# Resetting, at each batch item, the tally that shares PSUM evictions between ACT and DVE

## Chip, cores, metric

One core of a Trainium2 chip. The metric is the device time of one execution in microseconds (us), the median of several.

PE is TensorE, PEld its weight loads, DVE VectorE, ACT ScalarE, POOL GpSimd. "L581" in a profile line is a line of the program; where an experiment adds lines to the program, the same statement has a number a few higher or lower.

## The reference

Four batch items of 8 heads, 768 positions, head size 64. A Sinkhorn-normalised matrix P (8 by 8 per head) mixes blocks of K and V; block-local attention follows; its result goes through a two-branch layer:

```python
k_sorted = einsum('bhij,bhjcd->bhicd', P, k_b); v_sorted = einsum(... P, v_b)
attn = softmax(scale * q_b @ k_sorted^T)          # 96 x 96 blocks
x = (attn @ v_sorted) -> (B*S, H*D)               # 3072 x 512
out = maximum(x @ w1, x @ w2) @ w_out             # d_ff 1024
```

The kernel uses max(a, b) = max(a - b, 0) + b, so a hidden tile h needs a ReLU, and the second term becomes a product with wc = w2 @ w_out.

## The kernel before, where it matters

All matmul outputs, of every kind, use one PSUM pool of four buffers of 128 x 1024 fp32. Most evictions (PSUM to SBUF) may run on ACT or on DVE. `load` is a tally of estimated ns per engine, and `pick` takes the engine whose sum would be the lower. Work that is bound to one engine is added too.

```python
psum = ctx.enter_context(tc.tile_pool(name="psum", bufs=4, space=PSUM))  # 128 x 1024 fp32 each
load = {"A": 0.0, "D": 0.0}

def pick(a_ns, d_ns):
    if load["A"] + a_ns <= load["D"] + d_ns:
        load["A"] += a_ns
        return "A"
    load["D"] += d_ns
    return "D"

def evac(out_ap, in_ap, n, two_x=False, eng=None):
    a_ns, d_ns = (200 + n) / 1.2, (130 + (n / 2 if two_x else n)) / 0.96
    if eng:
        load[eng] += a_ns if eng == "A" else d_ns
    if (eng or pick(a_ns, d_ns)) == "A":
        nc.scalar.copy(out=out_ap, in_=in_ap)
    else:
        nc.vector.tensor_copy(out=out_ap, in_=in_ap)
# scores():  load["A"] += 800 (exp);  values(): load["D"] += 900;  turn(): load["D"] += 800
# moe_h():   the same pick, then a ReLU on ACT or a max on DVE
```

Items are pipelined: while item b goes through the hidden layer and the output product, item b+1 has its K and V sorted, its scores made and its attention applied. The loop of items (cut):

```python
for b in range(B):
    units = [lambda t=t: moe_h(b, 0, t, None if b else "A") for t in range(4)]
    ...                                   # the units of item b: h tiles, then outputs
    steps, lo = [], 2
    if b < B - 1:
        ...                               # the steps for item b+1: sort_k, sort_v, scores, values
        elif b == 1:
            vs = [lambda t=t: sort_v_pair(2, t) for t in range(8)]
            steps = group(*ks) + group(*vs[:2]) + group(*SC[0:2], late_loads)
            steps += group(*vs[2:4]) + group(*vs[4:6]) + group(*vs[6:]) + group(*SC[2:4]) + VA[:2]
    ...                                   # units and steps are issued in turn
```

Item 1 is thus where three K tiles and eight V tiles (V1 to V8) fall between eight h tiles. That stretch is what this document is about; its length is taken from the first K matmul to the first output matmul.

The softmax here doesn't subtract the row's maximum and nothing guards it: scores larger than these inputs give would overflow.

## Time and profile before

| | before |
|---|---|
| time | 173.48 us (173.47 to 173.84, 3 runs) |
| span in the profile | 171.4 us |
| TensorE busy | 161.7 us, 94% |
| ACT / DVE busy | 83.7 / 87.9 us |
| first K matmul to first output matmul of item 1 | 76.91 to 91.08: 14.17 us |

TensorE is busy 94% of the span, and a change that only moves evictions does not change its work, so only its waits can be won. Here is the end of the stretch, from the timeline of the kernel before (start, length, engine, line, operation):

```profile
91.08 1.25 PE L608 MATMUL out_ps<-wo_sb,g 128*128 128x512 bf16 x5
```

### The profile page before, as it was taken

Reading aid. Unit: us, or ns where it says so; the run is one execution under the profiler, and the core shown is the slowest. Engines: PE = TensorE matmul, PEld = TensorE weight load, DVE = VectorE, ACT = ScalarE, POOL = GpSimd, SP = SyncE. Lnnn points to the kernel's source line nnn. Section 1 sums busy time; section 2 is a strip of 40 time slices with the busy share of each in tenths; the row PEclk is TensorE's granted clock in tenths of the full one; section 3 lists DMA queues with packets and bytes.
Section 4 is the critical chain, followed back from the end, with each engine's and each line's share of the span. In section 5 each row is a group of like instructions: output and inputs, shape, how many; then the busy total and the mean of one; then the engine's idle time right before and its main releaser. Section 6 shows DMA issues by size and latency. Waiting matters only on the chain.

```text
span 171.4 us, 4548 instructions
## 1 busy us (share of the span) xinstructions
PE 161.7 (94%) x2015; PEld 96.6 (56%) x2015; DVE 87.9 (51%) x194; ACT 83.7 (49%) x102; POOL 24.8 (14%) x40
## 2 busy tenths in 40 slices
PE   7699999999999999998889999999999999999992
PEld 7548676736666554456555455575545445654462
DVE  5879668499556399810485644225472232420040
ACT  4599975846645554069764253275605214231001
POOL 7955362242300000000320000000000000000000
PEclk9999999999999999999999999999999999999999
DMA  4999999999999452992099267950023273000333
GB/s 49 201 205 207 199 207 206 207 205 207 213 222 196 76 168 54 193 232 96 4 174 189 54 168 145 195 183 4 2 50 77 91 205 130 6 0 0 122 122 126
DMA packets 29811, 23.11 MB, mean 135 GB/s; under 512 B 16672, under 2 KB 24736, under 8 KB 29792
## 3 DMA queue, kind: packets, MB, share of 16 engines
q0 software_dynamic: 10304, 12.58, 43.1%
q1 hardware_dynamic: 19200, 10.04, 23.2%
q8 instruction: 16, 0.26, 0.6%
q10 hardware_dynamic: 288, 0.20, 0.4%
q14 instruction: 3, 0.02, 0.0%
HBM read 25.17 MB, written 6.29 MB: 184 GB/s over the span
## 4 chain that ended last, share of the span: by engine, by line
PE 80%; DVE 10%; ACT 6%; issue 2%; DMA 1%; DVEq 0%; ACTq 0%
PE out_ps L608 37%; PE h_ps L581 22%; PE o_ps L471 4%; PE wc_ps L559 3%; PE k_ps L377 3%; PE s_ps L444 3%; ACT v_sb L103 2%; PE v_ps L398 2%; DVE v_sb L105 1%; ACT kT L103 1%; DVE x L488 1%; PE tw_ps L529 1%; PE tq_ps L347 1%; PE tq_ps L352 1%; ACT g L595 1%
## 5 line engine op out<-in xcount | busy, mean ns | idle before, releaser
L608 PE MATMUL out_ps<-wo_sb,g 128*128 128x512 bf16 (+2 forms) x208 | 48.3, 363 | 0.0
L581 PE MATMUL h_ps<-xT,w_sb 128*128 128x384 bf16 x256 | 44.8, 326 | 2.1 <-DVE v_sb L105 0.7
L581 PEld LDWEIGHTS <-w_sb 128*128 128x128 bf16 x256 | 24.2, 98 | 17.5 <-issue 2.0
L452 ACT ACTIVATE e<-s_ps 96x768 bf16<-96x768 f32 x32 | 24.2, 808 | 16.7 <-PE s_ps L444 16.6
L595 ACT ACTIVATE g<-h_ps 128x768 bf16<-128x768 f32 x23 | 18.6, 812 | 17.4 <-PE h_ps L581 17.4
L608 PEld LDWEIGHTS <-g 128*128 128x128 bf16 x208 | 17.6, 97 | 15.2
L608 PE MATMUL out_ps<-wc,xT 128*128 128x512 bf16 (+2 forms) x104 | 25.0, 362 | 0.0
L103 ACT COPY o<-out_ps 128x1024 f32<-128x1024 f32 x10 | 10.1, 1012 | 29.3 <-PE out_ps L608 24.7
L488 DVE TENSOR_TENSOR x<-o_ps,rs 96x512 bf16<-96x512 f32 x32 | 22.0, 687 | 1.1
L597 DVE TENSOR_SCALAR g<-h_ps 128x768 bf16<-128x768 f32 x9 | 8.6, 956 | 25.5 <-PE h_ps L581 25.5
L482 DVE RECIPROCAL rs<-o_ps 96x8 f32<-96x8 f32 x32 | 6.4, 200 | 21.4 <-PE o_ps L471 21.4
L608 PEld LDWEIGHTS <-xT 128*128 128x128 bf16 x104 | 9.9, 97 | 11.0
L471 PEld LDWEIGHTS <-e 96*128 96x128 bf16 x256 | 11.6, 98 | 6.9 <-DVE x L488 0.7
L209 DVE COPY v_dc<-v_raw 64x768 bf16<-64x768 bf16 (+2 forms) x18 | 15.4, 896 | 0.1
L471 PE MATMUL o_ps<-v_sb,e 96*128 96x65 bf16 x256 | 13.1, 193 | 0.3 <-DVE x L488 0.2
L105 DVE CAST v_sb<-v_ps 96x1024 bf16<-96x1024 f32 x7 | 8.3, 1214 | 4.1 <-PE v_ps L398 3.3
L103 ACT CAST v_sb<-v_ps 96x1024 bf16<-96x1024 f32 x9 | 8.8, 1020 | 1.6 <-PE v_ps L398 1.6
L444 PEld LDWEIGHTS <-kT 64*128 64x128 bf16 x256 | 6.1, 94 | 5.6 <-issue 4.8
L103 ACT CAST kT<-k_ps 128x1024 bf16<-128x1024 f32 x9 | 8.6, 1022 | 0.7 <-PE k_ps L377 0.7
L444 PE MATMUL s_ps<-qT,kT 64*128 64x96 bf16 x256 | 8.8, 204 | 0.2
L559 PE MATMUL wc_ps<-wo_sb,w2T 128*128 128x512 bf16 x32 | 7.7, 380 | 0.0
L81 PEld LDWEIGHTS <-fill 128*128 128x128 bf16 x109 | 6.3, 112 | 2.2 <-DVE fill L72 1.2
(76 smaller groups left out, 129.4 us busy)
## 6 DMA issues: line engine op xcount, KB each, us to landing
out_dram<-o SPq DMA_DIRECT2D x11, 512.0 KB, 3.0
k_raw<-in_k_dram POOLq DMA_DIRECT2D x12, 256.0 KB, 10.2
q_raw<-in_q_dram POOLq DMA_DIRECT2D x4, 768.0 KB, 12.5
v_raw<-in_v_dram POOLq DMA_DIRECT2D x6, 384.0 KB, 13.5
w_sb<-in_moe_w_dram POOLq DMA_DIRECT2D x3, 512.0 KB, 15.9
wo_sb<-in_moe_w_out_dram POOLq DMA_DIRECT2D x2, 512.0 KB, 19.2
v_raw<-in_v_dram POOLq DMA_DIRECT2D x3, 256.0 KB, 4.9
w_sb<-in_moe_w_dram POOLq DMA_DIRECT2D x2, 256.0 KB, 14.2
```

The lines of the kernel that those rows point to most:

```text
L103: nc.scalar.copy(out=out_ap, in_=in_ap)
L105: nc.vector.tensor_copy(out=out_ap, in_=in_ap)
L209: nc.vector.tensor_copy(out=dst, in_=src)
L444: nc.tensor.matmul(ps[:, h2 * 512 + ii * 128 : h2 * 512 + ii * 128 + BLK], kT[b][rows, (hp * 8 + i) * BLK : (hp * 8 + i) * BLK + 128], rhs ...
L452: nc.scalar.activation(out=e[:, 0 : 8 * BLK].rearrange("p (t c r) -> p t c r", t=8, r=R), in_=ps[0:BLK].rearrange("p (t f) -> p t f", t=8) ...
L471: nc.tensor.matmul(ps[:, h2 * 512 + ii * 65 : h2 * 512 + (ii + 1) * 65], e[:, (h2 * 4 + ii) * BLK : (h2 * 4 + ii) * BLK + 128], v_sb[:, m0 ...
L488: nc.vector.tensor_tensor(out=x, in0=ov[:, :, :, 0:D], in1=rs.to_broadcast([BLK, 2, 4, D]), op=ALU.mult,)
L559: nc.tensor.matmul(wc_ps[0][:, m * 512 : (m + 1) * 512], w2T[:, fb, dmt * 128 : (dmt + 1) * 128], wo_sb[:, fb, :], start=(fb == 0), stop=( ...
L581: nc.tensor.matmul(h_ps[t][:, m * 512 : m * 512 + TCH], w1_sb[:, hp, fb * 128 : (fb + 1) * 128], xT[:, b % 2, ch, hp % 2, hp // 2, :], sta ...
L595: nc.scalar.activation(out=g, in_=src, func=AF.Relu)
L597: nc.vector.tensor_scalar(out=g, in0=src, scalar1=0.0, scalar2=None, op0=ALU.max)
L608: nc.tensor.matmul(dst, g_tiles[b, ch, m // 2][:, m % 2, off : off + 128] if m < NFB else xT[:, b % 2, ch, hp % 2, hp // 2, off : off + 12 ...
```

## The change

The tally is meant to balance two engines, but it adds up from the start of the program, and a sum charged in one stage is paid back in another. The change starts it from zero at each item:

```diff
         steps, lo = [], 2
+        load["A"] = load["D"] = 0.0
         if b < B - 1:
```

No instruction is added; only which engine empties which tile changes. The choices of `pick` in order, before and after (A for ACT, D for DVE; those of item 0's tail, items 1, 2 and 3; the exps and copies that are bound to one engine are not among them):

```
item 0  before AAAAAADADADADDAAA        after AAAAAAAAADDADDAAA
item 1  before AAAAAAAAADDDAADADADAAA   after ADADADADADDADADAADAADA
item 2  before AAADADADADDAAA           after ADADADADADDAAA
item 3  before DADADAADAD               after ADADADADAD
```

## The prediction

> **What bounds the kernel now.** I read the page's first part, then the table of busy time by stretch, then what TensorE waited for, then the timeline of the one stretch in which TensorE isn't full. First the page: time busy, its share of the span, and instructions.
>
> ```profile
> PE 161.7 (94%) x2015; PEld 96.6 (56%) x2015; DVE 87.9 (51%) x194; ACT 83.7 (49%) x102; POOL 24.8 (14%) x40
> ```
>
> TensorE (PE) is the bound. The two engines that empty PSUM are half idle, so moving work between them gains nothing unless TensorE waits for one. TensorE idles 171.4 - 161.7 = 9.7 us. The table by stretch says where: per stretch its length, then busy us of PE, weight loads, DVE, ACT, POOL, the clock, DMA.
>
> ```profile
> 40.00:54.00 14.00, 13.65 (x244) 9.26 (x242) 8.96 (x11) 9.14 (x11) 1.44 (x2) 1.00 1.12 211
> 54.00:72.00 18.00, 18.00 (x180) 9.19 (x179) 14.22 (x30) 6.54 (x8) 0.00 (x0) 1.00 0.64 124
> 77.00:91.00 14.00, 12.07 (x296) 8.18 (x296) 5.83 (x6) 10.88 (x13) 2.67 (x5) 1.00 0.50 102
> 91.00:110.00 19.00, 19.00 (x178) 9.75 (x171) 8.76 (x19) 6.59 (x9) 0.00 (x0) 1.00 0.78 157
> 110.00:125.00 15.00, 14.64 (x220) 9.33 (x218) 6.20 (x9) 9.51 (x12) 0.00 (x0) 1.00 0.27 57
> ```
>
> From 54 to the output tail TensorE is full except from 77 to 91, where it lacks 1.93 us. There ACT is busy 10.88 of 14 us and DVE only 5.83: exactly the imbalance a tally should prevent. This is item 1 (the second of four): its hidden-layer tiles h, with item 2's sorted K (three tiles) and sorted V (eight) between them. The rest of the 9.7 us lies mostly ahead of 40 us (3.9 in the first two stretches of the same table) and after the last matmul, where no `pick` decides. TensorE's waits between 76.9 and 91.1:
>
> ```profile
> PE h_ps L581 <- DVE v_sb L105: 0.7, 1, 0.7
> PE h_ps L581 <- ACT v_sb L103: 0.6, 1, 0.6
> PE h_ps L581 <- ACT kT L103: 0.5, 1, 0.5
> ```
>
> These are matmuls waiting for an eviction unrelated to their operands: all PSUM tiles come from one pool of four buffers, so a tile starts when the tile four before it has been emptied. The timeline (start, length, what, idle before and its releaser) shows the queue behind it:
>
> ```profile
> 76.91 1.70 PE L377 MATMUL k_ps<-bd,k_raw 64*64 64x64 bf16 x96
> 77.01 0.81 ACT L595 ACTIVATE g<-h_ps 128x768 bf16<-128x768 f32 x1 [0.49 <-PE h_ps L581]
> 77.72 2.84 ACT L103 CAST kT<-k_ps 128x1024 bf16<-128x1024 f32 x3
> 79.69 1.46 PE L581 MATMUL h_ps<-xT,w_sb 128*128 128x384 bf16 x8 [0.51 <-ACT kT L103]
> 80.42 1.96 ACT L103 CAST v_sb<-v_ps 96x1024 bf16<-96x1024 f32 x2
> 82.42 1.46 PE L581 MATMUL h_ps<-xT,w_sb 128*128 128x384 bf16 x8 [0.57 <-ACT v_sb L103]
> 83.99 0.96 DVE L597 TENSOR_SCALAR g<-h_ps 128x768 bf16<-128x768 f32 x1 [10.25 <-PE h_ps L581]
> 84.87 3.47 DVE L105 CAST v_sb<-v_ps 96x1024 bf16<-96x1024 f32 x3
> 87.26 1.46 PE L581 MATMUL h_ps<-xT,w_sb 128*128 128x384 bf16 x8 [0.69 <-DVE v_sb L105]
> 114.43 2.36 DVE L105 CAST kT<-k_ps 128x1024 bf16<-128x1024 f32 x2 [6.19 <-PE k_ps L377]
> ```
>
> TensorE makes a K tile in 0.54 us (96 matmuls in 1.63 us, three tiles) and a V tile in 0.285 us (two in 0.57), but one eviction takes about 1.0 us on ACT or 1.2 on DVE. ACT takes nine evictions and two exps in a row while DVE idles 10.25 us; then DVE gets four in a row and TensorE waits for DVE. The last line is the same place one item later: there the tally was balanced, DVE took two of three K tiles, and TensorE did not wait.
>
> **Why the tally does this.** Each of item 0's turns of V charges DVE 800 ns, in a part of the kernel where TensorE does not wait. Worked through the code, the sums at the start of item 1 are ACT 35573, DVE 43021: a debt of 7447 ns, which ACT repays with the next nine picked evictions. For item 2 it is ACT 57013, DVE 58700; for item 3 ACT 71527, DVE 71110.
>
> **What the Trainium skill says.** "Perfetto Trace Analysis", Identifying the Most-Contended Engine, says that kernels can have regimes with different contended engines; the stretch table agrees (PE everywhere, evictions from 77 to 91). Its section Optimization Strategy says that the same gap repeating on the engine that should be saturated can mean too little PSUM for the next tile: three gaps of 0.5 to 0.7 us in 8 us, each released by an eviction, agree. "TensorEngine Tiling (Array Packing)", PSUM Bottleneck, advises using both ScalarE and VectorE for evacuation; the trace agrees that one alone can't keep up with 0.285 and 0.54 us tiles.
>
> **The change part by part.** It adds no instruction on the chip: both sums are set to zero while the program is built, at each item. The order of TensorE's instructions is identical. Only the engine of some evictions changes, found by comparing the built instruction orders; net, four go from ACT to DVE (DVE 183 to 187 counting sequencer rows).
>
> *Item 0's tail (43 to 53 us).* The reset comes before item 0's remaining picks, and DVE's charges lie ahead again: third K tile and second V tile go D to A, third V tile A to D. TensorE's two waits of 0.2 us there are for the first V tile's eviction and the weight product's copy, both on ACT as before. Gain 0. The moved V tile delays the Q copy on DVE by about 0.4 us, to end near 50.95; scores need it at 51.21. Cost 0.
>
> *Item 1's middle (73 to 91 us).* Engines, before then after, in tile order: h h h K K K V V h s s h V V h V V h V V h: A A A A A A A A A A A D D D A A D A D A D, becomes A D A D A D A D A A A D D A D A D A A D A. I replay it with durations from the trace: ACT h 0.81, K 1.02, V 1.00, exp 0.78; DVE h 0.96, K 1.19, V 1.2; ready 0.2 us after the last matmul; a buffer restarts 0.05 us after its eviction.
> - K1 on DVE 77.65 to 78.84, K2 on ACT 78.19 to 79.21, K3 on DVE 78.80 to 79.98 (before: 78.8, 79.6, 80.56).
> - V1 on ACT to 80.13, V2 on DVE to 81.2. The h tile behind V2 needs K2: starts 79.27, not 79.69.
> - It ends, two score tiles follow (K3's and V1's buffers are free), and the next h needs V2's buffer: 81.25, not 82.42. Gain so far 1.17.
> - V3, V4 at 82.64, 82.93; next h needs the second exp (83.1): starts 83.21, not 84.53. Gain 1.32.
> - V5, V6 at 84.61, 84.97 (needs V3, DVE until 84.93); next h at 85.30 needs V4, now on ACT until 84.38: no wait, where before it waited until 87.26. Gain 1.96.
> - V7, V8, h, two score tiles run without waits; the outputs begin at 89.12, not 91.08.
>
> So the stretch from 76.91 loses 1.96 us. As a check, its TensorE work alone is 1.63 (K) + 4 x 0.57 (V) + 5 x 1.40 (h with its switch) + 4 x 0.225 (scores) = 11.81 us against 14.17 now: at most 2.36 can be gained, and my replay keeps 0.4 of waits.
>
> *Item 1's outputs.* One output copy goes to DVE at 104.03 (1.22 us), ahead of a reciprocal and multiply that then end 1 us late. Four buffers and a spacing of 1.5 us absorb it. Cost 0.
>
> *Items 2 and 3.* One h of item 2 goes to DVE, which idles there 6 us. In item 3's eight h, the first six swap engines; each is made in 1.30 us and emptied in 0.81 or 0.96, so TensorE has no wait before or after. The wait of 0.3 us at 121.3 keeps its engines and stays. Gain 0.
>
> Sum: -1.96 us, none of it covered again, because TensorE is full from 91 to the end and everything there follows TensorE. 173.48 - 1.96 = 171.52, taken as 171.5.
>
> **Rivals.** (a) *Nothing*: evictions were hidden, or a transfer bounds the end of item 1. For: ACT 49%, DVE 51%. Against: three waits with named evictions, and DMA moves only 102 GB/s in this stretch, with the next item's loads issued behind its first exp and so earlier too. It would make 173.4. (b) *The wait changes hands*: DVE is slower per tile (1.2 to 1.0), and V2 or V6 on DVE becomes the releaser. For: the trace's largest wait, 0.69, is on DVE. Against: it followed four DVE evictions in a row; now never more than two. Half the gain would be left: 172.5. (c) *Later stages worsen*, because item 0's DVE charges or the output copy on DVE delay the attention chain. For: DVE carries 14.22 of 18 us from 54 to 72. Against: nothing moves onto DVE in that stretch. At most +0.5, so 172.0. (d) *Full gain*, no waits left: 173.48 - 2.36 = 171.1.
>
> **Range and chances.** (d) and (b) bracket it, with my replay nearer (d); I take 171.1 to 172.4. Over 2% needs 3.47 us, more than all the idle time of this stretch: 2%. Slower by 2% needs a new stall of 3.5 us where none is in sight: 1%. Within 2%: 97%.
>
> **What would show it.** In the changed kernel's trace: busy TensorE from 77 to 89 near 98%; the three waits gone or below 0.15 us each; ACT and DVE both between 8.5 and 10 us busy in that stretch (adding up the tiles above); first output matmul of item 1 near 89.1; all before 76.9 and the spacing after the stretch unchanged. A wait of TensorE on DVE's V eviction of over 0.5 us would prove (b); a new wait after 91 (c).

## The result, and the profile after

| | before | changed |
|---|---|---|
| time, median | 173.66 us (173.47 to 173.95, 4 runs) | 171.69 us (171.44 to 171.83, 4 runs) |
| ratio | | 0.9884 (95%: 0.9863 to 0.9904) |
| item 1, first K matmul to first output matmul | 76.91 to 91.08: 14.17 us | 77.03 to 89.11: 12.08 us |
| start of the program's last copy | 168.30 | 166.27 |

A ratio is the mean time of one kernel's fast runs over that of the other's from the same rounds, so not quite the ratio of the medians. The medians differ by 1.97 us. The interval is clear of 1.

The page's first line of the changed kernel: DVE has four instructions more and ACT four fewer, TensorE's share rises because the span shrank.

```profile
PE 162.8 (96%) x2015; PEld 97.5 (57%) x2015; DVE 91.7 (54%) x198; ACT 80.5 (47%) x98; POOL 24.6 (14%) x40
```

TensorE's busy time rose by 1.1 us without an instruction more: the first 13 us hold 11.00 us of it against 9.89, with the same 151 matmuls. Those are the fillers around the start, where the kernel waits for other things; busy time there is no progress.

Busy time by stretch in the changed kernel (length, then PE, PEld, DVE, ACT, POOL, clock, DMA):

```profile
40.00:54.00 14.00, 13.65 (x243) 9.28 (x242) 7.67 (x10) 10.17 (x12) 1.45 (x2) 1.00 1.12 211
54.00:72.00 18.00, 18.00 (x181) 9.21 (x179) 14.30 (x29) 6.54 (x8) 0.00 (x0) 1.00 0.64 122
77.00:89.00 12.00, 12.00 (x297) 8.05 (x296) 8.78 (x8) 8.89 (x11) 2.68 (x5) 1.00 0.55 113
89.00:108.00 19.00, 19.00 (x180) 9.77 (x173) 9.10 (x19) 6.02 (x9) 0.00 (x0) 1.00 0.82 164
108.00:123.00 15.00, 14.70 (x221) 9.33 (x219) 7.19 (x10) 8.72 (x11) 0.00 (x0) 1.00 0.28 57
```

The third line answers to the 14 us of before that lacked 1.93: the same work of TensorE (297 matmuls to 296) in 12 us, full, with ACT 8.89 and DVE 8.78 in place of 10.88 and 5.83. In the neighbouring stretches TensorE's busy time is as it was to within 0.06 us. The timeline of the same stretch:

```profile
77.77 2.36 DVE L105 CAST kT<-k_ps 128x1024 bf16<-128x1024 f32 x2 [0.97 <-PE k_ps L377]
78.27 1.01 ACT L103 CAST kT<-k_ps 128x1024 bf16<-128x1024 f32 x1 [0.32 <-PE k_ps L377]
79.39 1.47 PE L581 MATMUL h_ps<-xT,w_sb 128*128 128x384 bf16 x8
81.30 1.46 PE L581 MATMUL h_ps<-xT,w_sb 128*128 128x384 bf16 x8
83.27 1.48 PE L581 MATMUL h_ps<-xT,w_sb 128*128 128x384 bf16 x8
83.38 1.01 ACT L103 CAST v_sb<-v_ps 96x1024 bf16<-96x1024 f32 x1 [0.28 <-PE v_ps L419]
83.67 1.21 DVE L105 CAST v_sb<-v_ps 96x1024 bf16<-96x1024 f32 x1
85.28 1.47 PE L581 MATMUL h_ps<-xT,w_sb 128*128 128x384 bf16 x8
89.11 1.47 PE L608 MATMUL out_ps<-wo_sb,g 128*128 128x512 bf16 x6
```

The four h groups at 79.39, 81.30, 83.27 and 85.28 carry no wait that the profile lists. They are those of 79.69, 82.42, 84.53 and 87.26 before, of which three waited. V3 and V4 are now emptied side by side (83.38 on ACT, 83.67 on DVE), where before both stood in DVE's queue.

What TensorE waited for between 9 and 170 us of the changed kernel is down to seven waits of about 0.2 us, of which these three are behind an eviction by ACT:

```profile
PE h_ps L581 <- ACT g L595: 0.2, 1, 0.2
PE tq_ps L347 <- ACT wc L103: 0.2, 1, 0.2
PE tq_ps L347 <- ACT v_sb L103: 0.2, 1, 0.2
```

### The profile page after: what moved, and what is told of

It is laid out like the page before. It is cut to its first block, busy times and chain, and to the rows that moved or that the text cites. A ratio compares the mean times of both kernels' runs of the same rounds, so it can differ in the third digit from the quotient of the medians.

```text
span 169.9 us, 4550 instructions
## 1 busy us (share of the span) xinstructions
PE 162.8 (96%) x2015; PEld 97.5 (57%) x2015; DVE 91.7 (54%) x198; ACT 80.5 (47%) x98; POOL 24.6 (14%) x40
## 4 chain that ended last, share of the span: by engine, by line
PE 84%; DMA 7%; ACT 2%; POOL 2%; DVE 1%; issue 1%; POOLq 0%
PE out_ps L608 37%; PE h_ps L581 25%; DMA q_raw<-in_q_dram 7%; PE o_ps L471 5%; PE s_ps L444 4%; PE wc_ps L559 3%; PE k_ps L377 3%; PE v_ps L419 1%; PE tw_ps L529 1%; PE tq_ps L347 1%; PE tq_ps L352 1%; POOL k_raw L144 1%; POOL v_raw L153 1%; DVE x L488 1%; PE tx_ps L509 1%
## 5 line engine op out<-in xcount | busy, mean ns | idle before, releaser
L595 ACT ACTIVATE g<-h_ps 128x768 bf16<-128x768 f32 x21 | 16.9, 811 | 18.0 <-PE h_ps L581 18.0
L103 ACT COPY o<-out_ps 128x1024 f32<-128x1024 f32 x9 | 9.1, 1012 | 30.0 <-PE out_ps L608 25.7
L597 DVE TENSOR_SCALAR g<-h_ps 128x768 bf16<-128x768 f32 x11 | 10.5, 955 | 22.5 <-PE h_ps L581 22.5
L81 PEld LDWEIGHTS <-fill 128*128 128x128 bf16 x109 | 7.4, 125 | 2.2 <-DVE fill L72 1.2
L103 ACT CAST kT<-k_ps 128x1024 bf16<-128x1024 f32 x8 | 7.7, 1020 | 1.1 <-PE k_ps L377 1.1
L105 DVE COPY o<-out_ps 128x1024 f32<-128x1024 f32 x2 | 2.5, 1225 | 10.6 <-PE out_ps L608 9.5
```

The costliest lines, as they stand in the source:

```text
L81: nc.tensor.matmul(ps[:, 0:w], w0, fill[:, 0:w], start=True, stop=True)
L595: nc.scalar.activation(out=g, in_=src, func=AF.Relu)
L597: nc.vector.tensor_scalar(out=g, in0=src, scalar1=0.0, scalar2=None, op0=ALU.max)
```

## The experiments

My theory: all of the gain is made in item 1's stretch, because there evictions set TensorE's pace and were not side by side. The rivals: the gain is spread over the items; it comes from taking work off ACT as such; or a wait is only handed from one engine to the other. Ten kernels ran, and all gave the right result. "Stretch" is the length in the profile from the first K matmul to the first output matmul of item 1; it is one reading, but free of the jitter of the kernel's start and end, which is as large as some of the effects (one kernel's six runs lay between 171.45 and 172.37 us). Where the engines in the stretch are the same it repeats: 12.08 in four profiles, 14.17 in two. Kernels of different rounds are best compared by their ratios.

| kernel | time, us | before of the same rounds, us | ratio (95%) | stretch, us |
|---|---|---|---|---|
| before | 173.66 | | | 14.17 |
| changed | 171.69 | 173.66 | 0.9884 (0.9863 to 0.9904) | 12.08 |
| changed_again | 171.71 | 173.63 | 0.9891 (0.9871 to 0.9911) | 12.08 |
| only_item1 | 171.55 | 173.89 | 0.9870 (0.9852 to 0.9888) | 12.08 |
| all_but_item1 | 174.01 | 173.89 | 1.0005 (0.9990 to 1.0021) | 14.17 |
| k_to_dve | 172.41 | 173.89 | 0.9915 (0.9900 to 0.9930) | 12.88 |
| v4_to_act | 172.91 | 173.89 | 0.9949 (0.9935 to 0.9964) | 13.42 |
| k_and_v4 | 172.05 | 173.70 | 0.9901 (0.9885 to 0.9918) | 12.10 |
| half_debt | 172.07 | 173.70 | 0.9905 (0.9889 to 0.9921) | 12.45 |
| act_debt | 172.59 | 173.70 | 0.9934 (0.9922 to 0.9946) | 13.44 |
| all_act | 174.73 | 173.63 | 1.0065 (1.0045 to 1.0085) | 15.20 |
| split_three | 172.18 | 173.70 | 0.9912 (0.9899 to 0.9924) | 12.08 |

### Where the gain is made: only_item1 and all_but_item1

The picks are replaced by a fixed list, so that one item can have its engines of after and the rest those of before, and the other way round (shown for only_item1, the list split by item here, the removed lines cut).

```diff
+    picks = iter("AAAAAADADADADDAAA" "ADADADADADDADADAADAADA" "AAADADADADDAAA" "DADADAADAD")
     def pick(a_ns, d_ns):
-        if load["A"] + a_ns <= load["D"] + d_ns:
-            ...
+        return next(picks)
```

> The kernel before, with the engines of the changed kernel for the picked evictions of item 1 alone (items 0, 2 and 3 as before). My theory (all of the gain is made in item 1's middle): the whole gain, 2.0 us below the kernel before, near 171.65. Rival (the gain is spread, part of it from the swaps in items 0, 2 and 3): 1.0 us or less of it.

> The complement: the changed kernel's engines in items 0, 2 and 3, the engines of before in item 1. My theory: as before within 0.2 us, with the three TensorE waits of 0.5 to 0.7 us back in item 1. Rival (spread gain): 1.0 us or more below the kernel before.

Measured: item 1 alone makes the whole gain (0.9870; stretch 12.08), the other three items together none (1.0005; stretch 14.17, with its three waits back). The spread gain is excluded.

### Which moves make it: k_to_dve, v4_to_act, k_and_v4

Of the engines of before, only the named tiles are changed; the tally goes on as if they had not been (the diff is cut).

```diff
+    moved = {20: "D", 22: "D"}      # k_to_dve: K1, K3.  v4_to_act: {28: "A"}.  k_and_v4: all three
         if load["A"] + a_ns <= load["D"] + d_ns:
             load["A"] += a_ns
-            return "A"
+            return moved.get(picks["n"], "A")
```

> The kernel before, with only the first and third K tile of item 1's middle moved from ACT to DVE. My theory, replayed by hand with durations from the trace: the first two waits (0.51 and 0.57) go, DVE's queue of four still stands and keeps about 0.9 us of the third wait (V4 on DVE until about 85.9, the h tile ready at 85.06); in all 1.3 us below the kernel before, near 172.35. Rival (the DVE copy of K is slower, 1.19 to 1.02 us, so the wait only changes hands): 0.3 us or less.

> The kernel before, with only the fourth V tile of item 1's middle moved from DVE to ACT. My theory: the wait of 0.69 us on DVE goes and the first two stay; 0.7 us below the kernel before, near 172.95. Note that this move loads ACT, already the busier engine (10.9 to 5.9 us in this stretch): a rival that sees only the sums of work expects it slower or the same.

> Both single moves together: first and third K tile to DVE, fourth V tile to ACT, all else as before. My theory: three moves of the changed kernel's thirteen or so in item 1 make the whole gain, 2.0 us below the kernel before, near 171.65. Rival (the moves don't add, because clearing one wait uncovers another): 1.5 us or less.

Measured: 1.48, 0.98 and 1.65 us below the kernel before by the medians; by the stretch 1.29, 0.75 and 2.07. The expectations were 1.3, 0.7 and 2.0. The timeline of k_to_dve shows the first two waits gone and the third still behind DVE's queue of an h and three V tiles:

```profile
82.87 0.96 DVE L601 TENSOR_SCALAR g<-h_ps 128x768 bf16<-128x768 f32 x1 [2.70 <-PE h_ps L585]
83.75 3.47 DVE L109 CAST v_sb<-v_ps 96x1024 bf16<-96x1024 f32 x3
86.14 1.46 PE L585 MATMUL h_ps<-xT,w_sb 128*128 128x384 bf16 x8 [0.72 <-DVE v_sb L109]
```

That of v4_to_act shows the reverse: the first two waits stand, the third is gone.

```profile
79.82 1.46 PE L585 MATMUL h_ps<-xT,w_sb 128*128 128x384 bf16 x8 [0.51 <-ACT kT L107]
82.55 1.46 PE L585 MATMUL h_ps<-xT,w_sb 128*128 128x384 bf16 x8 [0.57 <-ACT v_sb L107]
86.62 1.47 PE L585 MATMUL h_ps<-xT,w_sb 128*128 128x384 bf16 x8
```

v4_to_act is the instructive one: it puts work on ACT, the engine that is busier in this stretch, and is faster. What counts here is which eviction stands behind which, not the sums. In the profile the two parts add (1.29 + 0.75 = 2.04, together 2.07), and three moved tiles do what the whole change does. The time of k_and_v4 says so less clearly: 1.65 us by the medians, 1.4 to 2.0 by the interval, which does not exclude the rival's 1.5. In its profile the transposes of Q near 17 us wait 0.30 us for the load of Q, which has nothing to do with the edit; but the changed kernel has 0.19 of that wait too, so it explains 0.1 of the 0.36 us between the two medians, and the rest is open.

### How much debt: half_debt, act_debt, all_act

```diff
         steps, lo = [], 2
+        if b == 1:
+            load["A"], load["D"] = 0.0, 3723.0     # half_debt.  act_debt: 7447.0, 0.0
```

In both debt runs the tally runs on, so some later picks, in item 3 and for act_debt in item 2 too, differ from those of before. all_act uses the fixed list with nineteen A at the start of item 1.

> The tally of item 1 starts with DVE charged 3723 ns, half of what it owes in the kernel before, in place of 0; no reset elsewhere. Replayed by hand: K1 and K2 stay on ACT, K3 and V2 go to DVE, V4 to ACT; the h tile behind the V pair still starts 0.1 us late, the next ones 0.7, 0.8 and 1.4 us earlier than before. 1.4 us below the kernel before, near 172.25. Rival (any debt that makes ACT start with two K tiles loses all): under 0.5 us.

> The debt turned round: item 1 starts with ACT charged 7447 ns and DVE 0, so DVE takes the first seven evictions. If the gain comes from splitting the evictions (my theory), this loses it: replayed by hand, the waits come back behind DVE and the outputs begin within 0.3 us of the kernel before, near 173.4. Rival (the gain comes from taking work off ACT, which still has the exps to do): as fast as the changed kernel or faster, 171.7 or below.

> All nineteen picked evictions of item 1 up to its outputs on ACT, everything else as before. My theory (in this stretch the queue of evictions sets TensorE's pace): ACT then has, from 77.01, one h, three K, eight V, five more h with the exps between them; added up in its order until V8 is out 16.2 us, so the outputs begin near 93.2 where the kernel before has 91.08, and the time is 2.1 to 2.5 us above the kernel before, near 175.9. Rival (the tally's distribution matters only through single unlucky waits, not through the sum of the work): under 1 us slower.

half_debt gained 1.63 us by the medians, 1.72 by the stretch: somewhat more than the 1.4 of my replay, and far from the rival's 0.5. Its one larger wait is the 0.51 us behind ACT's K copies, which the replay had too.

act_debt refutes the rival, as it is slower than the changed kernel by 0.9 us though it has less on ACT in the stretch (6.57 us busy against 9.00; DVE has 11.64). But my own number was wrong: it gained 1.11 us, not 0.3. The timeline:

```profile
77.94 3.47 DVE L105 CAST kT<-k_ps 128x1024 bf16<-128x1024 f32 x3
80.33 1.46 PE L581 MATMUL h_ps<-xT,w_sb 128*128 128x384 bf16 x8 [0.72 <-DVE kT L105]
81.33 1.21 DVE L105 CAST v_sb<-v_ps 96x1024 bf16<-96x1024 f32 x1
81.73 0.51 PE L444 MATMUL s_ps<-qT,kT 64*128 64x96 bf16 x16
82.59 1.46 PE L581 MATMUL h_ps<-xT,w_sb 128*128 128x384 bf16 x8 [0.35 <-DVE v_sb L105]
```

The first wait behind DVE is there. But the second score tile, which by "the tile four before" has to wait for V1 on DVE (81.33 to 82.54), starts without a wait in the group at 81.73. The built program shows why: the pool does not hand out its buffers strictly in turn. With V1 on DVE and V2 on ACT it gave the score tile V2's buffer and the h tile behind it V1's, and the order of buffers stays exchanged from there. So "the tile four before" holds in this stretch of the kernel before and of the changed kernel, whose buffers are the same throughout, but moving an eviction can move buffers too. The stretch accounts for 0.73 us of the 1.11. Another 0.21 us lie behind it in the profile: from the first output matmul to the last copy act_debt takes 77.01 us, the kernel before 77.22 and the changed one 77.16, with other buffers and other picks; which of the two does it is open, and so is the rest.

all_act is slower, by 1.10 us and 1.03 in the stretch, and its stretch shows the queue in pure form: DVE does nothing for 14 us, ACT is full, and TensorE waits 0.48 to 0.57 us before four of the five h tiles and before the first output.

```profile
77.00:91.00 14.00, 11.79 (x282) 7.92 (x282) 0.00 (x0) 13.96 (x18) 2.67 (x5) 1.00 0.54 109
```

It is half of the 2.1 to 2.5 us that I expected, and the times alone do not exclude the rival's "under 1 us" (0.8 to 1.5 us by the interval); that the queue paces TensorE here is read from the profile. I had added 16.2 us of ACT work until V8 is out; in the trace it took from 77.03 to 92.07, 15.04 us. The step from one eviction to the next is shorter than an instruction's row: the three K copies take 2.84 us as a row, but the next copy starts 2.70 us after the first, 0.90 us each, where the mean of one row is 1.02.

### Trying to go on: split_three

In the changed kernel three waits of TensorE behind an eviction are left. Each of those evictions is cut in halves for both engines (shown, with cuts: the weight product; the first V tile that is sorted during item 0 and one h tile of item 2 are cut alike).

```diff
-            evac(wc[:, dmt - 1 : dmt + 1, :]..., wc_ps[0], 1024, eng=eng)
+            if dmt == 3:
+                evac(wc[:, 2, :], wc_ps[0][:, 0:512], 512, eng="A")
+                evac(wc[:, 3, :], wc_ps[0][:, 512:1024], 512, eng="D")
```

> The changed kernel, with the three evictions that TensorE still waits for in items 0 and 2 (first V tile 0.16, weight product 0.19, one h tile of item 2 about 0.25 us) each cut in two halves, one for ACT and one for DVE. If TensorE's waits of this kind go into the time one for one (my theory), about 0.5 us below the changed kernel, 171.2, and the fastest of all. Rival: the two smaller instructions' fixed cost and the second semaphore eat it, 171.7.

It went the other way: 172.18 us, 0.4 to 0.5 above the changed kernel, whose nine runs (171.38 to 171.97) all lie below its four (172.01 to 172.26). The halves do not run side by side:

```profile
48.16 0.69 DVE L105 CAST v_sb<-v_ps 96x512 bf16<-96x512 f32 x1 [4.12 <-ACT v_sb L103]
48.90 0.83 PE L347 MATMUL tq_ps<-ident,q_pair 128*128 128x128 bf16 x12 [0.46 <-DVE v_sb L105]
118.70 0.49 ACT L608 ACTIVATE g<-h_ps 128x384 bf16<-128x384 f32 x1 [1.29 <-PE h_ps L594]
119.23 0.56 DVE L609 TENSOR_SCALAR g<-h_ps 128x384 bf16<-128x384 f32 x1 [0.28 <-ACT g L608]
119.83 1.46 PE L594 MATMUL h_ps<-xT,w_sb 128*128 128x384 bf16 x8 [0.48 <-DVE g L609]
```

In each pair the DVE half starts when the ACT half has ended, and the built program has a wait on ACT's semaphore in front of all three DVE halves. So the h tile is freed after 0.49 + 0.56 us and the gap between, later than after one copy of 0.81. TensorE's waits grew from about 0.2 to nearly 0.5 us each; at the weight product it was also that the pool gave the Q transposes another buffer than in the changed kernel, one that an exp on ACT had to free. It was in the trace of before for whoever looked: the one eviction that the kernel itself cuts in two, of the transposed w2, shows the same in its list of waits:

```profile
DVE w2T L105 <- ACT w2T L103: 1.0, 1, 1.0
```

My rival had the fixed cost and the second semaphore eat the gain; what the trace shows is an order between two engines that read the same PSUM tile. TensorE's waits did go into the time, but as a loss. This closes the idea of splitting a tile of this pool; two smaller tiles in its place were not tried. Two engines on two tiles, as V3 and V4 in the changed kernel, do run side by side.

changed_again, the control:

> The changed kernel itself once more, beside the others' chip and with more rounds than at first: 0.9884 of the kernel before as in the first comparison, 0.987 to 0.990, and the same stretch from the first K tile to the outputs, 12.08 us in the trace.

It held: 0.9891, and 12.08 us again. No experiment gave a version that is clearly faster than the changed kernel; only_item1 and k_and_v4 are the same thing by the stretch.

## Why the prediction was right

171.5 us was predicted, 171.69 measured; 1.96 us of gain, 1.97 measured by the medians and 2.09 in the stretch. The 0.19 us between the two times comes from the starting value: the kernel before had a median of 173.48 in the three runs known then, and has 173.66 in four. The signs that it named came too: TensorE 12.00 of 12 us busy, ACT 8.89, DVE 8.78, the outputs at 89.11.

- *The bound is TensorE, and only its waits can be won.* Right: the last copy of the program starts 2.03 us earlier, nearly what the stretch gained, so all that follows just moved forward.
- *The cause is a debt in the tally.* Right: only_item1, half_debt and the original change give 2.3, 1.6 and 2.0 us of gain with the debt of item 1 avoided by a list, halved and removed. A debt of the same size on ACT's side (act_debt) still gains 1.1, so what costs is not the debt's size but the evictions that it queues.
- *The steps of the replay.* The h groups came at 79.39, 81.30, 83.27 and 85.28, replayed 79.27, 81.25, 83.21 and 85.30; the outputs at 89.11, replayed 89.12. The changed kernel reached the stretch 0.12 us later than the kernel before (a wait of 0.19 us for the load of Q near 17 us lies ahead of it), so the gain within the stretch is 0.13 us larger than replayed. The replay kept 0.4 us above the 11.81 us of TensorE work; measured is 12.08, so 0.27 were kept, without a listed wait. Of these 0.15 lie in the first V pair, which takes 0.72 us to the next h tile where later pairs take 0.58 to 0.61.
- *Items 0, 2 and 3 give nothing.* Right (all_but_item1). The Q copy on DVE was delayed to end at 50.81, before its scores at 51.34, and the output copy on DVE at 102.06 delayed two multiplies and no matmul.
- *Rival (b), the wait changes hands.* Wrong as a forecast here, but real as a mechanism: act_debt, with all three K on DVE, has a new wait of 0.72 us behind them, and k_to_dve alone leaves the third wait behind DVE (0.72 us, 0.69 before). The change moves V4 off DVE in the same go, and v4_to_act shows that this takes the third wait away. The prediction's argument against (b), "now never more than two" DVE evictions in a row, was not the reason: it counts tiles in TensorE's order, while the four before were counted in DVE's queue, and in that count the changed kernel has four again (82.80 to 86.88, two h and two V). What matters is that TensorE's next tile did not need the last of them.
- *Rival (c), a later stage worsens.* Not seen: no new wait after 89 us.
- *What was weak in it.* The rule "the tile four before" was right for this stretch of these two kernels because their buffers are handed out alike; act_debt shows that it need not be so. "Full except from 77 to 91" overlooks the 0.36 us that its own table lacks from 110 to 125, of which 0.28 is the wait at 121.3; it became 0.22. And rows added up end to end overstate a full queue, as all_act shows; the changed kernel has no such queue.

## What to carry to other kernels

Read busy time by stretch, not over the span: two engines at half load can hide a stretch where one queue paces TensorE and the other engine idles. A balance by running sums can repay old charges at the wrong place; let it forget at the border of a stage, or perhaps better, though not tried here, ask which engine is free when the tile is ready. And the order of evictions can count more than their sum: moving one V tile onto the busier engine won 0.98 us by the medians and 0.75 in its stretch, and cutting a tile between both engines lost time, because its halves ran one after the other.

## What the Trainium skill lacked or had wrong

- "TensorEngine Tiling (Array Packing)", PSUM Bottleneck, advises both ScalarE and VectorE for evacuation, but not how: two tiles on two engines overlap (83.38 and 83.67 us in the changed kernel), the two halves of one tile do not (split_three: the DVE half at 119.23 after the ACT half of 118.70 to 119.19).
- "PSUM — Partial Sum Buffer", PSUM bank collisions raise a hardware error, tells of dependencies between engines on the same bank and quadrant. The halves in split_three start 512 fp32 columns apart, by that page's size of a bank in two different banks, and the build still ordered them, at a cost of about 0.3 us per wait. No page says that the build keeps this order per tile.
- No page has it that a pool may hand out its PSUM buffers in another order when an eviction changes engine: in act_debt two tiles exchanged buffers, and the stretch was 13.44 us where my replay in strict order came to about 14.
- "Perfetto Trace Analysis", Optimizing Scalar/DVE Operations, says that half of an instruction's access latency overlaps with the next one, and puts this overhead for ScalarE at about 93 ns on SBUF and 51 ns on PSUM; it has no figure for a copy from one to the other. The runs agree that rows overlap: ACT's K copies in a queue advance by 0.90 us where a row has 1.02, an overlap of 0.12 us.
